# A list scheduler's model of TensorE waves, tile changes and GpSimd results is changed, with its margin and its table of moods

## The chip, the cores and the metric

The kernel runs on one NeuronCore of a Trainium2 chip. The metric is the time of one execution on the device in microseconds (us). Smaller is better. Times are medians of several executions of the same built kernel; a profile is taken of one execution.

## The reference

The input `x` has 2048 tokens of 512 numbers. Two layers follow each other, each with an attention part A and a mixer-and-MLP part B. Part A has 32 heads of 16 numbers that share one key and one value projection. Biases and gains are absent everywhere.

```python
def _A_ref(x, wq, wk, wv, wo):                     # H = 32, Dh = 16
    q = (x @ wq) -> (heads, 2048, 16); k = x @ wk; v = x @ wv
    p = softmax(q @ k.T * Dh ** -0.5)              # 32 x 2048 x 2048
    return concat_heads(p @ v) @ wo
def _B_ref(x, w1, w2, w3, w4):
    h = gelu(layernorm(x) @ w1)                    # 512 wide, four parts of 128
    hs = (parts of h shifted by +1, -1, +2, -2 tokens) @ w2
    x1 = x + hs
    return x1 + gelu(layernorm(x1) @ w3) @ w4      # 1792 wide
x = x + A(layernorm(x)); x = x + B(layernorm(x))   # twice
```

The exponentials are the largest elementwise work: 2 layers x 32 heads x 2048 x 2048 = 268 million of them.

## The kernel before

**Tiling.** Tokens are cut into 16 tiles of 128. A chunk is four tiles (512 queries); in the second layer the last chunk is cut in two of 256 queries (`CHUNKS`). Attention of a chunk is done in eight blocks of four heads, each over 16 key tiles. The unit of attention is a *half*: two heads, 512 query columns, one key tile (two key tiles for a chunk of 256), so 2 x 512 scores on 128 partitions. There are 2048 halves in the kernel.

**Two ways for a half.** `declare_unit` (L1099) has TensorE write the scores QK into two PSUM banks (L1071), and ScalarE (ACT) take the exponential of 128x1024 in one instruction, L1115, into `EA`. TensorE then multiplies it by the values (the PV product, L1194, from `EA`). Two pairs of PSUM banks are used in turn, so ACT can work on one half while TensorE fills the next. `declare_pair` (L1121) does the exponential without ACT: VectorE (DVE) turns the scores into the bits of a bf16 number by a multiplication and an addition (`J`, L1136, two per half). Two more versions with another step added (`JK`, L1146) are made by GpSimd (POOL), or by DVE when POOL already has `ADDS` of them open. The PV product then takes `J` and two `JK`, three times the PV work of a unit.

**PV on TensorE.** A PV product is four matmuls in four column strips of the array, which run side by side: one *wave*. All dense products (projections W1, W2, W3, W4, WO through `dot`, L670) are waves of four matmuls as well. QK uses row strips, and two to four QK matmuls run side by side. A change from row strips to column strips, or to the whole array, is a *tile change*.

**What sets the order.** Nothing is ordered by hand. The program first builds a list of operations with estimated durations, and the class `Plan` plays them through in its own clock: at each moment it picks, for every free engine, the ready operation of the best priority. The order that comes out is emitted as five in-order instruction streams with semaphore waits; at run time only the order is left, not the planned times. What the planner believes sits in constants and in `_place` (L321): an operation may start `LAT` (60 ns for TensorE) after its producer's planned end. TensorE's side work, which is all of it but QK and PV, starts `MARGIN` later still, and takes a freed PSUM bank only `MARGIN` after the planned end of what freed it (`_after`, L158, `_pick`, L197); QK and PV (`side=False`) have no margin. A change of kind on TensorE costs `SWITCH` (`begin`, L271). A TensorE operation of `stream` columns lasts `stream / 2400` us at the full clock. QK for ACT has priority 0 and is protected by due times (`limits`, L282); PV has 2 and, in the side work of projections and MLPs, priorities go up to 12. When TensorE's planned activity falls short, `filler` (L1077) puts in a wave of zeros, ONES times NIL (L670), which keeps the array's clock up. `pump` and `assign` decide which halves go to DVE and POOL.

**The table.** `TEMPER` has one symbol for each 12.5 us of planned time. `temper` (called by `pump`) reads it and sets eight rules of the planner (`RULES`) to one of 16 rows of `MOODS`.

**Other streams.** SP issues all DMAs; eight small ones (L1280, OT<-OS) move each finished block's output to where the output projection WO reads it. For the last three blocks of a layer TensorE does that instead (L1270). ACT also does the gelus of the mixer (L1455) and of the MLP (L1535), each between two table loads.

The names that matter below: L1115 (EA, ACT), L1071 (QK), L1194 (PV), L670 (all dense waves), L1136 and L1146 (J and JK), L1280 (block outputs by DMA), L1535 (MLP gelu).

Of the kernel before, what the change touches and what calls it, by code (L numbers as in the profile page):

```python
# [31 lines left out]
class Plan:  # L32
# [6 lines left out]

    DRAIN = {"ACT": 0.15, "DVE": 0.085, "POOL": 0.0}  # L40
    SELF = 0.035
    MARGIN = 0.15
    SWITCH = 0.097
    WINDOW = 3.4133
    WARM = 0.40
    STAY = 0.36
# [111 lines left out]
    def _after(self, p, o):  # L158
# [5 lines left out]
        if o.eng == "PE" and o.side:  # L164
            lat += self.MARGIN
        elif o.side:
# [30 lines left out]
    def _pick(self, eng, t, dense=False):  # L197
# [15 lines left out]
        for o in h:  # L213
# [6 lines left out]
            if limit and o.prio > 0:  # L220
                end = self.run_end(o, t)
                if (not joins or end > self.pe_end + 0.02) and \
                        any(end + (self.SWITCH if o.pe[0] != "Q" else 0.0) > x for x in limit):
                    continue
# [3 lines left out]
            if self.CLOSE and eng == "PE" and o.prio > 2 and o not in low and o.take is None:  # L228
                key = (self.CLOSE, o.seq)
            if stick and o.prio > 2 and o.pe[0] == self.pe_kind and not any(self.run_end(o, t) + self.SWITCH > x for x in due):  # L230
                key = (self.STICK, o.seq)
# [5 lines left out]
            if o.take is not None:  # L237
                if not all(p.placed and (p.end <= t + 1e-9 or p.eng == "PE") for p in o.take.gates):
                    continue
                margin = self.MARGIN if o.side else self.LAT["PE"]  # L240
                for i, (ft, b) in enumerate(self.pool):
# [29 lines left out]
    def begin(self, o, t):  # L271

        if o.pe[0] != self.pe_kind:
            return max(t, self.pe_end + self.SWITCH)
        if len(o.pe) == 3:
# [32 lines left out]
    def lend(self, banks, o):  # L308

        for b in banks:  # L310
            self.pool.append((o.end, b))
            self.pool_last[b] = o
        heapq.heappush(self.events, o.end + self.MARGIN)

# [6 lines left out]
    def _place(self, o, t):  # L321
        o.start = t
        o.placed = True
        if o.port and o.eng == "POOL" and o.dur > 0.5:
            x = self.order["DVE"][-1] if self.order["DVE"] else None
            if x is not None and x.port and x.start <= t < x.start + self.RACE and len(self.order["DVE"]) > 1:
                o.preds.add(self.order["DVE"][-2])
        self.left -= 1
        o.pos = len(self.order[o.eng])
        self.order[o.eng].append(o)  # L330
        if o.dma:
            s = max(t + 0.61 * (o.parts - 1) + 1.4, self.dma_free)
            o.end = s + o.dma / 330e3 + 0.6
            self.dma_free = s + o.dma / 330e3
            self.free_at[o.eng] = t + 0.63 * o.parts
        elif o.eng == "PE":
            self.roll(t)
            kind, stream, act = o.pe[0:3]
            f = 2400.0 if self.warm else 1200.0
            o.start = t = self.begin(o, t)  # L340
            end = t + stream / f
            if kind != self.pe_kind:
                self.lane = [t] * 4
            for x in (o.pe[3] if len(o.pe) > 3 else range(4)):
                self.lane[x] = end
            self.pe_kind = kind
            self.pe_end = max(self.pe_end, end)
            o.dur = end - t
            o.end = end + 0.17
            self.free_at["PE"] = t + 0.015 if len(o.pe) > 3 else end  # L350
            heapq.heappush(self.events, self.pe_end)
            self.roll(self.pe_end)
            self.activity[-1] += act
            self.debt += self.KEEP * 2400.0 * (self.pe_end - self.debt_at) - act
            self.debt = min(max(self.debt, -self.CREDIT * 2400.0), self.CAP * 2400.0)
            self.debt_at = self.pe_end
        else:
            wait = 0.0
            if o.port:
                if o.eng == "DVE":  # L360
                    if self.port > t + 0.07:
                        wait = max(0.0, self.port + min(o.dur, self.BODY) - t - o.dur)
                    self.port = t + wait + o.dur
                else:
                    if o.dur > 0.5:
                        wait = max(0.0, self.port - 0.06 - t)
                    else:
                        wait = max(0.0, self.port - t)
                    self.port = t + wait + o.dur - (0.08 if o.dur > 0.5 else 0.0)
            self.free_at[o.eng] = t + wait + o.dur  # L370
            o.end = t + wait + o.dur - o.after + self.DRAIN[o.eng]
        heapq.heappush(self.events, self.free_at[o.eng])
        if o.give is not None:
            self.pool.append((o.end, o.give.bank))
            self.pool_last[o.give.bank] = o
            heapq.heappush(self.events, o.end + self.LAT["PE"])
            heapq.heappush(self.events, o.end + self.MARGIN)
        if o.feeds is not None and self.attach is not None:
            self.attach(o)
        for s in o.succ:  # L380
            s.npend -= 1
            r = self._after(o, s)
            if r > s.ready:
                s.ready = r
            if s.npend == 0:
                self._push(s)
        o.succ = None
# [112 lines left out]
def t_ps(n):  # L500
    return 0.066 + n * 1.043e-3


def t_x4(n):
    return 0.068 + n * 0.26e-3
# [18 lines left out]
class Kernel:  # L524
# [52 lines left out]
        (0.55, 3.0, 1.5, 3.0, 0.7, 1.2, 3, 6),  # L577
        (0.57, 2.0, 1.0, 2.0, 0.45, 1.0, 3, 4),
    )
    TEMPER = "9332e03ff77e3fffe9027e99e39c23f70e32017eeecfd1e2e715170b07f0d0890399f73cf77e47e749020d9f11791007e2af395f7507bce5"  # L580

    def __init__(self, nc, ins, out):
        self.stretch = -1
# [493 lines left out]
    def filler(self):  # L1077
# [4 lines left out]
        L = None  # L1082
        if self.main_done or dep is not None and not (dep.placed and dep.end + self.pl.MARGIN <= self.pl.now):
            if not any(t + self.pl.MARGIN <= self.pl.now for t, b in self.pl.pool):
                return
# [35 lines left out]
    def declare_pair(self, g):  # L1121

        op = self.pl.op
        m = self.ndve
        self.ndve += 1
        self.waiting.append(m)
        js = m % self.N_J
        J = self.J[:, js, :]  # L1130
        for i in range(2):
            h = 2 * g[5] + i
            L = Late()
            op("PE", lambda e, h=h, L=L: self.qk(e, g, h, L.bank), reads=self.inputs(g), writes=[L],
               pe=("Q", 512, 128, (h,)), prio=0.5, side=False, take=L)
            o = op("DVE", lambda e, i=i, L=L: e.tensor_scalar(  # L1136
                out=J[:, i * 512:(i + 1) * 512], in0=self.PB[:, L.bank, :],
                scalar1=128 * LOG2E * 0.25, scalar2=float(127 * 128), op0=ALU.mult, op1=ALU.add),
                writes=[L, ("J", js, i)], dur=t_ps(512), prio=1, side=False, give=L)
        jt = [("J", js, 0), ("J", js, 1)]  # L1140
        es = [(J, jt)]
        for k in (1, 2):
            r = (2 * m + k - 1) % self.N_JK
            self.adds = [p for p in self.adds if not p.placed]
            eng = "POOL" if len(self.adds) < self.ADDS else "DVE"
            x = op(eng, lambda e, k=k, r=r: e.tensor_scalar(  # L1146
                out=self.JK[:, r, :], in0=J, scalar1=float(self.STEPS[k]), scalar2=1.0, op0=ALU.add,
                op1=ALU.mult),
               reads=jt, writes=[("JK", r)], dur=t_x4(1024) if eng == "DVE" else 1.12, prio=2, side=False, port=True)
            if eng == "DVE":  # L1150
                o = x
            else:
                self.adds.append(x)
            es.append((self.JK[:, r, :], [("JK", r)]))
        self.pairs.append(o)
        self.add_pv(g, [(self.shaped(ap.bitcast(dt.bfloat16), [2, 512]), tg, k, m) for k, (ap, tg) in enumerate(es)])
# [136 lines left out]
    def temper(self, now):  # L1293
# [3 lines left out]
        self.stretch = w  # L1297
        mood = self.MOODS[int(self.TEMPER[w], 36) if w < len(self.TEMPER) else 0]
        for name, v in zip(self.RULES, mood):
# [302 lines left out]
```

## Time and profile before

| | us |
|---|---|
| median of 5 runs | 1506.49 |
| lowest and highest of the 5 | 1502.97 and 1508.63 |
| the profiled execution | 1506.16 |
| its span from first to last instruction | 1504.4 |
| TensorE busy (PE) | 1482.1 |
| ScalarE busy (ACT) | 1436.9 |
| VectorE busy (DVE) | 1335.1 |
| GpSimd busy (POOL) | 1218.0 |

A group of instructions is written as line, engine, operation, output<-input, shapes and number, then busy time and the mean length of one in ns, then how long the engine had been idle just before such instructions and which producer ended most of that idle time. In a timeline each row is a run of equal instructions: start, length, engine, line, and in brackets the idle time ahead of it with what ended it. Two cautions: matmuls are pipelined, and the record of a short one is longer than the time it occupies; and a row that merges several ACT instructions ends with the last one's end.

### The profile page before, as it was taken

The numbers are of one execution on the slowest core, as the hardware profiler recorded it, in microseconds if no ns is written. First come the engines' busy times: TensorE is split into PE (matmuls) and PEld (weight loads), VectorE is DVE, ScalarE is ACT, GpSimd is POOL, SyncE is SP. The second block draws the span as 40 slices with busy tenths as digits, with TensorE's granted clock in tenths as the row PEclk, the third lists the DMA queues.
The fourth block names the chain that finished last, engine by engine and source line by source line (L and its number), as shares of the span: only waits on it lengthen the run. The fifth ranks groups of instructions, "written<-read, shape, count | busy, mean of one in ns | idle before, by whom it ended". The sixth has DMA issues, their size and how long they took to land.

```text
span 1504.4 us, 63139 instructions
## 1 busy us (share of the span) xinstructions
PE 1482.1 (99%) x28473; PEld 652.2 (43%) x28473; DVE 1335.1 (89%) x2396; ACT 1436.9 (96%) x1519; POOL 1218.0 (81%) x1280
## 2 busy tenths in 40 slices
PE   9999999999999999999999999999999999999999
PEld 4444333444444444444444344444443435454555
DVE  8899999988999999998786899999799999898873
ACT  7999999999999999999989999999999999998962
POOL 3899989888899878998655797889789998787851
PEclk9999999999999999999999999999999999999999
DMA  6100100001000000100000000010000000000000
GB/s 212 29 6 6 20 6 6 6 3 21 5 6 5 5 7 5 19 4 2 2 3 3 2 9 9 7 20 5 13 14 8 5 6 14 14 11 8 8 14 24
DMA packets 32142, 21.50 MB, mean 14 GB/s; under 512 B 12672, under 2 KB 31360, under 8 KB 31872
## 3 DMA queue, kind: packets, MB, share of 16 engines
q1 hardware_dynamic: 31872, 17.47, 4.8%
q8 instruction: 222, 3.64, 1.0%
q14 instruction: 48, 0.39, 0.1%
HBM read 7.90 MB, written 2.10 MB: 7 GB/s over the span
## 4 chain that ended last, share of the span: by engine, by line
PE 53%; ACT 38%; DVE 6%; POOL 1%; issue 1%; DMA 0%
ACT EA L1115 37%; PE PB L1071 17%; PE PB L1194 17%; PE PB L670 16%; DVE J L1136 3%; PE PB L867 1%; POOL JK L1146 1%; ACT G L1535 1%; DVE ST L785 1%; PE PB L1000 1%; PE PB L1251 1%; DVE JK L1146 0%; PE PB L1236 0%; ACT L1115 0%; DVE Y L822 0%
## 5 line engine op out<-in xcount | busy, mean ns | idle before, releaser
L1115 ACT ACTIVATE EA<-PB 128x1024 bf16<-128x1024 f32 x1429 | 1323.3, 1074 | 13.2 <-PE PB L1071 9.7
L1146 POOL TENSOR_SCALAR JK<-J 128x1024 uint16<-128x1024 uint16 x1019 | 1081.2, 1061 | 191.7 <-DVE J L1136 95.8
L1136 DVE TENSOR_SCALAR J<-PB 128x512 uint16<-128x512 f32 x1238 | 796.3, 680 | 74.4 <-PE PB L1071 70.1
L1071 PE MATMUL PB<-QT,KT 32*128 32x512 bf16 (+1 forms) x4608 | 606.4, 360 | 6.7 <-ACT EA L1115 3.5
L1194 PE MATMUL PB<-EA,VP 128*32 128x256 bf16 (+1 forms) x6432 | 373.0, 264 | 1.3 <-DVE ACCF L1224 0.2
L1194 PE MATMUL PB<-JK,VD 128*32 128x256 bf16 (+1 forms) x5568 | 321.4, 265 | 2.7 <-POOL JK L1146 1.4
L1071 PEld LDWEIGHTS PB<-QT,KT 32*128 32x128 bf16 x4608 | 160.8, 91 | 358.6 <-ACT EA L1115 226.5
L1194 PEld LDWEIGHTS PB<-EA,VP 128*32 128x32 bf16 x6432 | 154.6, 95 | 131.1 <-issue 100.0
L1194 PEld LDWEIGHTS PB<-JK,VD 128*32 128x32 bf16 x5568 | 126.8, 94 | 155.6 <-issue 92.0
L1194 PE MATMUL PB<-J,VD 128*32 128x256 bf16 (+1 forms) x2784 | 174.2, 263 | 0.8 <-DVE J L1136 0.7
L670 PE MATMUL PB<-ZT,W 128*32 128x512 bf16 (+2 forms) x2816 | 167.8, 342 | 0.4 <-DVE ZT L876 0.2
L1146 DVE TENSOR_SCALAR JK<-J 128x1024 uint16<-128x1024 uint16 x219 | 149.9, 690 | 5.0 <-PE PB L1194 3.6
L670 PE MATMUL PB<-W,G 128*32 128x512 bf16 x1624 | 102.5, 380 | 0.1
L1194 PEld LDWEIGHTS PB<-J,VD 128*32 128x32 bf16 x2784 | 68.0, 95 | 38.1 <-issue 26.8
L1530 DVE CAST G<-PB 128x512 bf16<-128x512 f32 (+2 forms) x126 | 72.4, 581 | 12.2 <-PE PB L670 10.5
L670 PE MATMUL PB<-ONES,NIL 128*32 128x512 bf16 x800 | 75.0, 394 | 2.7 <-DVE J L1136 1.9
L670 PEld LDWEIGHTS PB<-ZT,W 128*32 128x32 bf16 x2816 | 65.1, 96 | 28.9 <-issue 16.1
L1535 ACT ACTIVATE G<-G 128x1792 bf16<-128x1792 bf16 x29 | 47.0, 1686 | 21.6 <-DVE G L1530 21.6
L805 POOL TENSOR_TENSOR SM<-SM,MH 128x2 f32<-128x2 f32 (+1 forms) x69 | 50.2, 729 | 21.4 <-DVE SM L807 10.5
L670 PEld LDWEIGHTS PB<-W,G 128*32 128x32 bf16 x1624 | 39.0, 96 | 37.1 <-issue 8.7
L1257 DVE TENSOR_TENSOR OS<-ACCF,PB 128x512 bf16<-128x512 bf16 (+1 forms) x72 | 44.4, 617 | 4.4 <-PE PB L1251 3.9
L1511 POOL TENSOR_TENSOR X<-Y,X 128x512 f32<-128x512 bf16 x32 | 37.6, 1180 | 8.5 <-DVE Y L1493 6.0
(108 smaller groups left out, 842.5 us busy)
## 6 DMA issues: line engine op xcount, KB each, us to landing
OT<-OS SPq DMA_DIRECT2D x424, 8.0 KB, 1.8
W<-in_B_w_dram SPq DMA_DIRECT2D x2, 1792.0 KB, 15.0
X<-in_A_x_dram SPq DMA_DIRECT2D x8, 256.0 KB, 4.9
QT<-QS SPq DMA_DIRECT2D x32, 64.0 KB, 2.5
out_dram<-OUTB SPq DMA_DIRECT2D x16, 128.0 KB, 1.7
OT<-OS SPq DMA_DIRECT2D x104, 4.0 KB, 1.8
W<-in_B_w_dram SPq DMA_DIRECT2D x2, 512.0 KB, 9.7
WQ<-in_A_wq_dram SPq DMA_DIRECT2D x1, 512.0 KB, 4.5
```

Source lines behind the costliest of these rows:

```text
L670: ins = e.matmul(self.PB[32 * g:32 * g + 32, bank, 0:n], lhsT=lhsT[:, 32 * g:32 * g + 32], rhs=rhs, start=start, stop=stop, tile_position= ...
L785: op("DVE", lambda e, tb=tb: e.bn_stats(self.ST6[:, tb, :], src(tb)), reads=[tagf(tb)], writes=[("ST", tb)], dur=0.606, prio=prio)
L805: op("POOL", lambda e: e.tensor_tensor(out=out, in0=src, in1=self.MH[:, 0, a:b], op=ALU.pow), reads=tags + [("MH",)], writes=tg(r), dur=0. ...
L1071: ins = e.matmul(self.PB[:, bank, j * n:(j + 1) * n], lhsT=self.KT[32 * h:32 * h + 32, la, (kb + j) * 128:(kb + j + 1) * 128], rhs=self.QT ...
L1115: o = q.feeds = op("ACT", lambda e: e.activation(self.EA[:, ea, :, :], self.PB[:, b0:b0 + 2, :], ACTF.Exp, scale=0.25), writes=bk + [("EA" ...
L1136: o = op("DVE", lambda e, i=i, L=L: e.tensor_scalar(out=J[:, i * 512:(i + 1) * 512], in0=self.PB[:, L.bank, :], scalar1=128 * LOG2E * 0.25 ...
L1146: x = op(eng, lambda e, k=k, r=r: e.tensor_scalar(out=self.JK[:, r, :], in0=J, scalar1=float(self.STEPS[k]), scalar2=1.0, op0=ALU.add, op1 ...
L1194: ins = e.matmul(self.PB[32 * x:32 * x + 32, self.ACC, p * hw:p * hw + hw], lhsT=v[:, la, kb + j, :], rhs=ap[:, i, j * w + u * hw:j * w + ...
L1257: op("DVE", lambda e: e.tensor_tensor(out=osm, in0=acc, in1=self.PB[:, M.bank, 0:n], op=ALU.mult), reads=am, writes=[M] + om, dur=t_ps(n), ...
L1511: op("POOL", lambda e, tb=tb: e.tensor_tensor(out=self.X32[:, tb, :], in0=self.Y[:, tb % 6, :], in1=self.X32[:, tb, :], op=ALU.add), reads ...
L1530: op("DVE", lambda e, f=f, L=L: e.tensor_copy(self.G2[:, f, 0:n], self.PB[:, L.bank, 0:n]), writes=[L] + [(x, f, i) for x in ("G2", "GE") ...
L1535: op("ACT", lambda e, i=i: e.activation(self.G2[:, :, i * 128:(i + 1) * 128], self.G2[:, :, i * 128:(i + 1) * 128], ACTF.Gelu_apprx_tanh), ...
```

## The change

Four constants or terms of the planner change, and the table.

- A PV or other column-strip operation (kind "P") lasts 6 ns longer in the plan for every 512 columns begun (`WAVE`).
- A tile change costs 103 ns in the plan in place of 97 (`SWITCH`).
- The margin kept ahead of TensorE's side work, and before side work uses a freed PSUM bank or a lent one comes in, falls from 150 to 90 ns (`MARGIN`).
- The result of a `JK` on GpSimd counts as ready 70 ns before the planned end of the instruction (`after`); DVE's `JK` is as before.
- `TEMPER` is another string, of 113 symbols in place of 112; past its end the first row of `MOODS` holds.

The arithmetic, the tiles, the buffers and the operations themselves are not touched; only their order and the choice between units, pairs, POOL and DVE can differ.

```diff
-    MARGIN = 0.15
-    SWITCH = 0.097
+    MARGIN = 0.09
+    SWITCH = 0.103
+    WAVE = 0.006
...
             kind, stream, act = o.pe[0:3]
             f = 2400.0 if self.warm else 1200.0
             o.start = t = self.begin(o, t)
-            end = t + stream / f
+            end = t + stream / f + (self.WAVE * ((stream + 511) // 512) if kind == "P" else 0.0)
...
-    TEMPER = "9332e03ff77e3fffe9027e99e39c23f70e32017eeecfd1e2e715170b07f0d0890399f73cf77e47e749020d9f11791007e2af395f7507bce5"
+    TEMPER = "8033ee39ee377177e2fc0e03ec3fe7470c0ad17fee0e5df7ee7330e00050000a42037e4ce5591f07513f43f3fee2df192097e373cc00f03c4"
...
-               reads=jt, writes=[("JK", r)], dur=t_x4(1024) if eng == "DVE" else 1.12, prio=2, side=False, port=True)
+               reads=jt, writes=[("JK", r)], dur=t_x4(1024) if eng == "DVE" else 1.12, prio=2, side=False, port=True,
+                   after=0.0 if eng == "DVE" else 0.07)
```

## The prediction, as put on record before the run

> **What bounds the kernel now.** I read the page first. PE is busy for 99% of the span, ACT for 96%.
>
> ```profile
> PE 1482.1 (99%) x28473; PEld 652.2 (43%) x28473; DVE 1335.1 (89%) x2396; ACT 1436.9 (96%) x1519; POOL 1218.0 (81%) x1280
> ...
> L1115 ACT ACTIVATE EA<-PB 128x1024 bf16<-128x1024 f32 x1429 | 1323.3, 1074 | 13.2 <-PE PB L1071 9.7
> ...
> L670 PE MATMUL PB<-ONES,NIL 128*32 128x512 bf16 x800 | 75.0, 394 | 2.7 <-DVE J L1136 1.9
> ```
>
> PE's 99% can't be taken at its word: 800 of its matmuls are 200 waves of zeros, put in where the planner saw room. ACT's 96% is real work. So I read ACT's timeline next, for where ACT stands still.
>
> ```profile
> 34.55 192.01 ACT L1115 ACTIVATE EA<-PB 128x1024 bf16<-128x1024 f32 x209 [0.66 <-PE PB L1071]
> ...
> 776.96 1.28 ACT L1535 ACT_TABLE_LOAD   x1
> 785.65 4.87 ACT L1535 ACTIVATE G<-G 128x1792 bf16<-128x1792 bf16 x3 [7.41 <-DVE G L1530]
> ...
> 794.82 16.30 ACT L1115 ACTIVATE EA<-PB 128x1024 bf16<-128x1024 f32 x17 [1.05 <-PE PB L1071]
> 812.13 7.53 ACT L1115 ACTIVATE EA<-PB 128x1024 bf16<-128x1024 f32 x8 [1.02 <-PE PB L1194]
> ...
> 1375.48 1.03 ACT L1115 ACTIVATE EA<-PB 128x1024 bf16<-128x1024 f32 x1 [3.22 <-PE PB L1071]
> ...
> 1384.02 60.11 ACT L1115 ACTIVATE EA<-PB 128x1024 bf16<-128x1024 f32 x64 [0.48 <-PE PB L1194]
> 1444.15 1.28 ACT L1455 ACT_TABLE_LOAD   x1
> ```
>
> From 34.55 to 1444.15 ACT stands still in two places only: at the change of layer (7.41 + 1.05 + 1.02 = 9.5 us) and near 1375 (3.22, then 0.72, 0.50 and 0.48: 4.9 us). After the last exponential come 60 us in which PE works alone.
>
> There is a third loss that the brackets don't show. Where nothing is late, exponentials start 0.906 us apart: in two narrow windows of the same view the first start is at 102.63 and at 107.16, five starts later (4.53 / 5).
>
> ```profile
> 102.63 5.67 ACT L1115 ACTIVATE EA<-PB 128x1024 bf16<-128x1024 f32 x6
> ...
> 107.16 6.65 ACT L1115 ACTIVATE EA<-PB 128x1024 bf16<-128x1024 f32 x7
> ```
>
> The 209 above take 192.01 / 209 = 0.919 each. Start by start, 762 of about 1400 are within 1 ns of 904; 218 are 41 to 300 ns later, together 21.5 us; another 338 are 2 to 20 ns later, 5.3 us, mostly right behind a late one. The late ones are late QKs. For 167 of the 218 (15.8 us) no wait of PE on DVE or POOL lies in the time before: PE simply came round too late. The other 51 (5.6 us) follow a PE wait, on POOL's JK above all (3.1 us).
>
> [...] The trace has this run of 26 waves:
>
> ```profile
> 729.04 5.79 PE L670 MATMUL PB<-W,G 128*32 128x512 bf16 x104
> ```
>
> Less one lone wave of 0.394 that is (5.79 - 0.394) / 25 = 0.216[...]. So the old plan, with 213.3, is 2.5 ns short per wave, and the new one, with 219.3, 3.5 long. A tile change costs 0.10 (QK start at 602.56, PV at 602.88, less 0.213), so 97 and 103 are both near. [...] the mean clock granted is 0.51 only from about 1375 to 1378, right behind PE's stall at 1371.
>
> **The change, part by part.** The built orders can be counted. Durations are those above; the sum is made against the profiled 1506.16, which is 0.3 below the median.
>
> (a) Work. EA goes from 1429 to 1430: +0.9 us on ACT. DVE gets 3 JK at 0.690 more and 2 J at 0.680 less, POOL 5 JK less: under 6 us, beside ACT, no cost. PE has 8 PV waves, 8 runs of QK and 41 waves of zeros less (200 to 159). At 0.216 the zeros are 8.9 us of PE time. By themselves they gain nothing, as ACT bounds; they count in (e). If ACT's cover were gone, the 8.9 would be the gain.
>
> (b) Change of layer. ACT's order tells it. Before: chunk 2's gelu G x4, EA x13, last chunk's GP gelu, EA x27, G x3, EA x27, G x2. After: GP, EA x1, G x4, EA x2, G x3, EA x31, G x2, with 21 EA more ahead of GP. So chunk 2's W4 now falls between G x4 and G x3. PE must do, from the first of the four gelus: 56 waves W4 (12.1 us), 56 waves W3 of 384 columns (9.1, at 0.163 from the run of 224 in the before trace, 9.28 long), 20 transposes with their tile changes (1.5), 9 PV (1.0), and DVE 0.8 for the last eviction: 24.5. ACT has meanwhile 4.85 of gelu, two table loads (2.56), two EA (1.84): 9.3. It stands still 15.2, against 9.5: **+5.7**. Bounds: 0 (PE work overlaps the gelu more than I see) to +9.
>
> (c) The stall near 1375. It is a WO that waits for block outputs by DMA:
>
> ```profile
> 1374.21 0.62 PE L670 MATMUL PB<-WO,OT 128*32 128x512 bf16 x8 [3.26 <-issue]
> ```
>
> and SP's queue shows why:
>
> ```profile
> 1323.26 49.73 SPq L1280 DMA_DIRECT2D OT<-OS  x64
> ```
>
> All eight blocks of the chunk sit in one queue: 64 issues at 0.78 us, where the plan counts 0.63. In the old order four of these blocks end within two halves of each other. In the new one the eight ends are some 7 to 13 us apart, and a block needs 8 x 0.78 = 6.2 us of SP; WO comes about 15 us after the last end. So the stall goes: **-4.9**. What is late next there is nothing that I find; bounds -4.9 to -2.
>
> (d) The end. Columns that PE must still stream after the last QK: 134,408 before, 141,320 after (80 more matmuls of chunk 2's W3, fewer W1 and PV). 6912 / 2400 = **+2.9**. PE has no slack there (56.0 us of streaming in the 61.8 that were left). Bounds +1 to +4.
>
> (e) Late QKs. WAVE and SWITCH make the plan charge for time that PE does need, so fewer side waves go ahead of a QK than fit. I take two thirds of the 15.8 away (-10.5) and of the small ones -2.0. Against it: JK of POOL has no margin at all. Before, the plan has it usable 1.12 + 0.06 = 1.18 after its start; now 1.11; in the trace it is 1.047 long and the waiting weight load starts 0.053 later: 1.10. The slack falls from 80 to 10 ns, while POOL's pitch in the trace is 1.125 to 1.175. I let the 3.1 us behind POOL double: +3.1. What queues behind a waiting PV is all of PE: the next QK, and behind it ACT. MARGIN concerns side work only; a DVE result then has 0.685 + 0.06 + 0.09 = 0.835 in the plan against 0.680 + 0.053: still 100 ns to spare, no cost; bounds 0 to +2. Net **-9.4**, bounds -19 to +8.
>
> Sum: 0.9 + 5.7 - 4.9 + 2.9 - 9.4 = -4.8. 1506.2 - 4.8 = 1501.4, or 1501.7 against the median; I say **1501.5**, by itself 1495 to 1503.4. A difference under 0.2% (3 us) is about what this measurement can't tell from none.
>
> **Rivals.**
> *Given back.* The late QKs lose only about 5 us and just pay for (b) and (d): 1506. For it: part (e) is the only large gain that is not a single event. Against: 15.8 us is precisely PE being later than planned.
> *Slower, by POOL.* PV waits for JK in order. If the waits behind POOL grow by more than 2 x 3.1 while the late ones without a wait fall by less than a third (-5), (e) is above +1 and the sum +5.6 or more: 1512, up to 1517. It decides from the point where (e) is above -1.6, the sum being then +3. For it: PE already waits for POOL often, with 80 ns of slack.
>
> ```profile
> PEld PB L1194 <- POOL JK L1146: 39.5, 153, 0.6
> ```
>
> Against it: each such wait is 0.26 us with the tile change in it, and most don't reach ACT.
> *It does not do what it says.* The plan now overcharges waves by 3.5 ns, so PE runs ahead of plan and the new table was fitted to a slower PE; ACT's starts stay as they are: 1506.2 + 4.6 = 1510.8.
>
> **How the numbers follow.** Forecast (faster) 0.50; given back 0.20; slower by POOL 0.17; not as said 0.13. Range 1492 to 1513: it takes in the bounds of (b) and (e) and most of the two slower cases. Faster 0.50, same 0.20, slower 0.30.
>
> **What would show it.** (a) 1430 EA. (b) One bracket of 13 to 17 us before the G x3 near 790, in place of 7.41. (c) No WO waiting on issue near 1375, SP's runs of L1280 of 8 to 16. (d) 62 to 65 us from the last EA to the end. (e) Mean pitch in long runs of EA at 0.910 to 0.914 in place of 0.919, and the wait of L1194 for POOL above 39.5. A pitch still at 0.919 makes the forecast wrong, and so does a half-clock stretch, since 41 waves of zeros are gone.

## The result and the profile after

| | before | after |
|---|---|---|
| median, us | 1505.46 (46 runs, 1502.89 to 1508.63) | 1502.34 (26 runs, 1502.05 to 1503.24) |
| ratio, 95% interval | | 0.998 (0.9975 to 0.9985) |
| the profiled execution | 1506.16 | 1502.23 |
| its span | 1504.4 | 1500.3 |
| exponentials on ACT (EA) | 1429 | 1430 |
| waves of zeros | 200 | 159 |

The change makes the kernel 3 us (0.2%) faster, and its times lie closer together (why is told under e2). In the code after, lines are one higher than before from L43 on and two higher from about L1152 on: QK is L1072, EA L1116, PV L1196, dense waves L671, JK L1147, the MLP's gelu L1537.

The groups of the page after, in the order in which those of before were shown:

```profile
PE 1477.9 (99%) x28277; PEld 654.5 (44%) x28277; DVE 1329.3 (89%) x2397; ACT 1429.8 (95%) x1520; POOL 1213.7 (81%) x1275
...
L1116 ACT ACTIVATE EA<-PB 128x1024 bf16<-128x1024 f32 x1430 | 1316.3, 1145 | 5.4 <-PE PB L1072 3.1
```

The shares of busy time say nothing of the gain. The idle time in the last line does: ACT was idle ahead of exponentials for 13.2 us before, for 5.4 after. ACT's timeline shows where it still stands:

```profile
769.28 1.28 ACT L1537 ACT_TABLE_LOAD   x1
786.22 4.87 ACT L1537 ACTIVATE G<-G 128x1792 bf16<-128x1792 bf16 x3 [15.66 <-DVE G L1532]
...
794.83 10.46 ACT L1116 ACTIVATE EA<-PB 128x1024 bf16<-128x1024 f32 x11 [0.48 <-PE PB L1072]
806.80 16.60 ACT L1116 ACTIVATE EA<-PB 128x1024 bf16<-128x1024 f32 x18 [1.51 <-PE PB L1196]
...
1375.32 56.19 ACT L1116 ACTIVATE EA<-PB 128x1024 bf16<-128x1024 f32 x61
1431.95 5.61 ACT L1116 ACTIVATE EA<-PB 128x1024 bf16<-128x1024 f32 x6 [0.44 <-PE PB L1196]
1437.58 1.28 ACT L1457 ACT_TABLE_LOAD   x1
```

The bracket at the change of layer has grown from 7.41 to 15.66 us. The stall near 1375 is gone: 61 exponentials run through it without a bracket. The next table load after the last exponential comes at 1437.58, not at 1444.15.

What the brackets don't show is the lateness of single starts. Over the whole kernel I took, for each exponential that follows another, how much more than 904 ns lies between the two starts, and summed what is under 300 ns. Call this the lateness. It fell from 29.3 to 19.2 us, and the starts that are 41 to 300 ns late fell from 218 to 135. The view of waits gives the same from PE's side. Its columns are the total in us, the number of waits and the longest. These are the weight loads of QK that wait for ACT to give a bank back, that is, QKs that are early. First before, then after:

```profile
PEld PB L1071 <- ACT EA L1115: 226.5, 743, 0.8
...
PEld PB L1194 <- POOL JK L1146: 39.5, 153, 0.6
```

```profile
PEld PB L1072 <- ACT EA L1116: 295.1, 1006, 0.8
...
PEld PB L1196 <- POOL JK L1147: 38.9, 152, 0.5
```

QK waits for ACT 1006 times instead of 743: PE is in front of ACT more often. PE's waits for POOL are unchanged.

The two profiled executions differ by 3.9 us, their spans by 4.0. The parts, from the two traces:

| part | us |
|---|---|
| first exponential starts at 13.51, not 14.18 | -0.7 |
| three brackets near its start, 1.56 in place of 2.21 | -0.6 |
| one exponential more | +0.9 |
| change of layer: 15.66 + 0.48 + 1.51 in place of 7.41 + 1.05 + 1.02 + 0.42 | +7.7 |
| from 1370 to the last exponential: 0.44 in place of 3.22 + 0.72 + 0.50 + 0.48 | -4.5 |
| lateness, 19.2 in place of 29.3 | -10.1 |
| from the last exponential to the end, 62.8 in place of 60.2 | +2.5 |
| not placed | +0.8 |
| sum | -4.0 |

The lateness that is won (-10.1) and what is lost at the change of layer and at the end (+7.7 and +2.5) cancel. What is left is about the size of the stall that went.

### The profile page after: what moved, and what is told of

Its sections match the earlier page's. It is cut to its first block, busy times and chain, and to the rows that moved or that the text cites. A ratio compares the mean times of both kernels' runs of the same rounds, so it can differ in the third digit from the quotient of the medians.

```text
span 1500.3 us, 62760 instructions
## 1 busy us (share of the span) xinstructions
PE 1477.9 (99%) x28277; PEld 654.5 (44%) x28277; DVE 1329.3 (89%) x2397; ACT 1429.8 (95%) x1520; POOL 1213.7 (81%) x1275
## 4 chain that ended last, share of the span: by engine, by line
ACT 70%; PE 24%; DVE 4%; POOL 1%; issue 0%; POOLq 0%
ACT EA L1116 67%; PE PB L671 10%; PE PB L1072 6%; PE PB L1196 6%; DVE J L1137 2%; ACT G L1537 1%; POOL JK L1147 1%; ACT L1116 1%; PE PB L868 1%; ACT GP L1457 1%; DVE JK L1147 1%; PE PB L925 0%; ACT L1457 0%; ACT L1537 0%; DVE G L1532 0%
## 5 line engine op out<-in xcount | busy, mean ns | idle before, releaser
L1116 ACT ACTIVATE EA<-PB 128x1024 bf16<-128x1024 f32 x1430 | 1316.3, 1145 | 5.4 <-PE PB L1072 3.1
L1147 POOL TENSOR_SCALAR JK<-J 128x1024 uint16<-128x1024 uint16 x1014 | 1077.1, 1062 | 167.3 <-DVE J L1137 82.5
L1072 PE MATMUL PB<-QT,KT 32*128 32x512 bf16 (+1 forms) x4608 | 610.3, 359 | 12.3 <-ACT EA L1116 6.1
L1196 PE MATMUL PB<-EA,VP 128*32 128x256 bf16 (+1 forms) x6448 | 370.1, 263 | 1.4 <-DVE ACCF L1230 1.0
L1072 PEld LDWEIGHTS PB<-QT,KT 32*128 32x128 bf16 x4608 | 163.3, 91 | 375.0 <-ACT EA L1116 295.1
L1196 PE MATMUL PB<-JK,VD 128*32 128x256 bf16 (+1 forms) x5536 | 318.9, 266 | 2.5 <-POOL JK L1147 1.5
L1196 PEld LDWEIGHTS PB<-EA,VP 128*32 128x32 bf16 x6448 | 154.8, 95 | 121.3 <-issue 93.7
L1196 PEld LDWEIGHTS PB<-JK,VD 128*32 128x32 bf16 x5536 | 126.8, 94 | 151.9 <-issue 91.8
L1196 PE MATMUL PB<-J,VD 128*32 128x256 bf16 (+1 forms) x2768 | 175.3, 264 | 0.2 <-DVE J L1137 0.2
L671 PE MATMUL PB<-ZT,W 128*32 128x512 bf16 (+2 forms) x2816 | 167.6, 342 | 0.7 <-DVE J L1137 0.2
L1147 DVE TENSOR_SCALAR JK<-J 128x1024 uint16<-128x1024 uint16 x222 | 143.9, 654 | 3.2 <-PE PB L1196 1.0
L671 PE MATMUL PB<-W,G 128*32 128x512 bf16 x1624 | 103.1, 380 | 0.1
L1196 PEld LDWEIGHTS PB<-J,VD 128*32 128x32 bf16 x2768 | 67.8, 95 | 42.1 <-issue 34.5
L671 PEld LDWEIGHTS PB<-ZT,W 128*32 128x32 bf16 x2816 | 65.1, 96 | 33.0 <-issue 17.0
L1537 ACT ACTIVATE G<-G 128x1792 bf16<-128x1792 bf16 x29 | 47.0, 1686 | 32.7 <-DVE G L1532 32.6
L806 POOL TENSOR_TENSOR SM<-SM,MH 128x2 f32<-128x2 f32 (+1 forms) x69 | 49.2, 716 | 21.0 <-DVE SM L808 10.1
L671 PE MATMUL PB<-ONES,NIL 128*32 128x512 bf16 x636 | 58.1, 401 | 0.1
L671 PEld LDWEIGHTS PB<-W,G 128*32 128x32 bf16 x1624 | 41.4, 96 | 34.3 <-issue 9.2
```

The source lines that it names most:

```text
L671: ins = e.matmul(self.PB[32 * g:32 * g + 32, bank, 0:n], lhsT=lhsT[:, 32 * g:32 * g + 32], rhs=rhs, start=start, stop=stop, tile_position= ...
L806: op("POOL", lambda e: e.tensor_tensor(out=out, in0=src, in1=self.MH[:, 0, a:b], op=ALU.pow), reads=tags + [("MH",)], writes=tg(r), dur=0. ...
L1072: ins = e.matmul(self.PB[:, bank, j * n:(j + 1) * n], lhsT=self.KT[32 * h:32 * h + 32, la, (kb + j) * 128:(kb + j + 1) * 128], rhs=self.QT ...
L1116: o = q.feeds = op("ACT", lambda e: e.activation(self.EA[:, ea, :, :], self.PB[:, b0:b0 + 2, :], ACTF.Exp, scale=0.25), writes=bk + [("EA" ...
L1147: x = op(eng, lambda e, k=k, r=r: e.tensor_scalar(out=self.JK[:, r, :], in0=J, scalar1=float(self.STEPS[k]), scalar2=1.0, op0=ALU.add, op1 ...
L1196: ins = e.matmul(self.PB[32 * x:32 * x + 32, self.ACC, p * hw:p * hw + hw], lhsT=v[:, la, kb + j, :], rhs=ap[:, i, j * w + u * hw:j * w + ...
```

## The experiments

The theory is that of the prediction: the constants let PE come to its QKs in time, the change of layer and the end give much of it back, and the stall near 1375 goes because the output projection WO no longer waits for the SP queue, which issues the DMAs. The rivals are that the new table was only a luckier order, that POOL's waits take part of the gain, and that the zeros matter. Experiments e1 to e4, e7 and e8 keep the order on every engine, so that only the named cost changes. In e5, e6 and e9 to e12 the planner runs with other constants and gives another order.

### The constants or the table: e5 and e6

The two diagonals of the change: the constants of after with the table of before, and the reverse.

```diff
-    MARGIN = 0.15   SWITCH = 0.097   (no WAVE, JK of POOL after=0.0)
+    MARGIN = 0.09   SWITCH = 0.103   WAVE = 0.006, JK of POOL after=0.07
     TEMPER of before                                      # e5; e6: the reverse
```

> The constants of after (margin 0.09, tile change 0.103, wave 0.006, POOL's JK 0.07 later) with the table of before. The program it builds has 1448 exponentials on ACT (before 1429), so the time must be about 19 x 0.92 = 17 us above before plus whatever the side work stalls: 1520 to 1550. The time is not the question, the lateness of starts is. Theory (the constants make the QKs come in time, whatever the table): lateness under 300 ns, summed over all starts of exponentials, near that of after, 18 to 22 us, with 120 to 150 starts 41 to 300 ns late. Rival (the new table was simply a luckier order, the constants do nothing to the lateness): near that of before, 27 to 31 us with 200 to 230 late starts.

> The constants of before with the table of after, the other diagonal. It builds with 1456 exponentials on ACT, 27 more than before: 25 us above before plus stalls, 1525 to 1550. Theory (constants make the lateness): 27 to 31 us of lateness under 300 ns and 200 to 230 starts 41 to 300 ns late, as before. Rival (the table makes it): 18 to 22 us and 120 to 150, as after.

Both are slower: e5 1568.47 us, ratio 1.0418 (1.04 to 1.0437), e6 1535.84 us, ratio 1.0205 (1.0188 to 1.0222). e5 is further off than expected: beside 19 exponentials more, ACT's brackets above 0.3 us between 35 us and the last exponential sum to 54.9 us against 14.8 before. But the lateness follows the constants: 19.6 us with 131 late starts in e5, 32.1 us with 243 in e6, which is a little above the 31 and 230 that were named for it. The waits of QK for ACT say the same, e5 first:

```profile
PEld PB L1072 <- ACT EA L1116: 286.5, 981, 0.8
```

```profile
PEld PB L1071 <- ACT EA L1115: 229.2, 735, 0.8
```

981 is like after's 1006, 735 like the 743 of before, whichever table is used. For the lateness the theory holds, and the luckier order falls; these two runs don't say whose doing the other parts of the ledger are. What the table does is another thing: it fits one set of constants, and with the other set the plan takes 19 or 27 more exponentials on ACT. e5 also stalls more (the 54.9 us above), e6 does not (13.4). So the time of a change of one part alone measures mainly the misfit.

### Which constant: e9 to e12

Each changes one of the four in the kernel before, with the old table.

```diff
+    WAVE = 0.006                                          # e9
-    SWITCH = 0.097
+    SWITCH = 0.103                                        # e10
-    MARGIN = 0.15
+    MARGIN = 0.09                                         # e11
-    dur=t_x4(1024) if eng == "DVE" else 1.12, prio=2, side=False, port=True)
+    dur=..., port=True, after=0.0 if eng == "DVE" else 0.07)   # e12
```

> The kernel before with WAVE alone (6 ns more per column-strip wave in the plan), old table. It builds with 1470 exponentials on ACT, so its time is 38 us above before plus stalls, 1540 to 1580; read is the lateness of starts (before 29.3 us under 300 ns, 218 starts 41 to 300 ns late). Theory, as in step (e) of the prediction: WAVE is the larger of the two corrections and brings most of what both constants bring, 20 to 24 us and 130 to 180 late starts. Rival (the margin does it): 27 to 31 us, 200 to 230.

> The kernel before with SWITCH alone (tile change 0.103 in place of 0.097), old table; 1471 exponentials on ACT, 1540 to 1580 us. Theory, as in step (e): it takes part of the lateness away, less than WAVE: 24 to 28 us, 180 to 210 late starts. Rival (it does nothing): 29 to 31 us.

> The kernel before with MARGIN alone (0.09 in place of 0.15), old table; 1470 exponentials on ACT, 1540 to 1580 us. Step (e) gave the margin no cost and no gain (0 to +2 us): 29 to 31 us of lateness, 210 to 235 late starts. Rival (side work that starts earlier leaves the QK's way sooner): 20 to 25 us. Second rival (the smaller margin puts PE behind DVE more often): above 33 us.

> The kernel before with the earlier result of POOL's JK alone (0.07), old table; 1468 exponentials on ACT, 1540 to 1580 us. Step (e) had the waits behind POOL double: PE's waits for POOL from 39.5 to 60 us or more and the lateness from 29 to 32 us or more. Rival (the waits behind POOL are as they were, because POOL's instruction itself is 1.05 to 1.07 where the plan has 1.12): 36 to 43 us of waits for POOL, lateness 28 to 30 us.

One execution each. The expectations had counted ACT's table loads with the exponentials; the traces have 1453 to 1457.

| kernel | time, us | lateness, us | starts 41 to 300 ns late | waits of QK for ACT | PE waits for POOL's JK, us |
|---|---|---|---|---|---|
| before | 1506.16 | 29.3 | 218 | 743 | 39.5 |
| e9 WAVE | 1556.77 | 23.1 | 138 | 930 | 40.3 |
| e10 SWITCH | 1554.56 | 23.4 | 163 | 882 | 26.5 |
| e11 MARGIN | 1553.87 | 32.0 | 243 | 712 | 32.6 |
| e12 POOL | 1552.29 | 30.1 | 227 | 714 | 41.0 |
| e5 all four | 1569.6 | 19.6 | 131 | 981 | 41.1 |
| after | 1502.23 | 19.2 | 135 | 1006 | 38.9 |

WAVE takes 6.3 us of lateness away and SWITCH 5.9; MARGIN adds 2.7 and POOL's term 0.8. Their sum, -8.7, is near the -9.7 of e5, so the four nearly add up. How far can one such number be trusted? The order of before was profiled twice more with other parts cut (e1, e2): 28.0 and 28.6; that of after once more (e3): 18.6. So one order varies by about 1 us from run to run. A new order is a new draw, and the table alone shows how wide that is: e6 has the constants of before and 2.8 us more lateness than before, e5 those of after and 0.4 us more than after. The 6 us of WAVE and of SWITCH are outside of this. The 2.7 of MARGIN and the 0.8 of POOL's term are not, so neither is shown to cost anything. WAVE came out as expected; SWITCH as strong as WAVE, where less was expected; MARGIN a little above the range named for it; and in e12 the waits for POOL did not double.

### The zeros: e1

In the kernel before, the last 175 of the 200 waves of zeros stream 32 columns instead of 512.

```diff
+        z = 512 if self.nfill < 25 else 32
...
-            "PE", lambda e: self.dot(e, ..., 512, self.NIL, self.ONES,
+            "PE", lambda e: self.dot(e, ..., z, self.NIL, self.ONES[:, 0:z],
```

> The kernel before with its order untouched; of the 200 waves of zeros the last 175 stream 32 columns instead of 512. PE gets back about 175 x 0.19 = 33 us, spread over the run. Theory (ACT bounds, and a QK is late because PE comes round late): the zeros stand where PE had room, so only a part of the late QKs profits. The 21.5 us of late starts fall to 15 to 19, the time by 2 to 5 us, 1501 to 1504. Rival 1 (the zeros keep the clock up): half-clock stretches appear and the time rises by over 3 us. Rival 2 (late QKs have nothing to do with how full PE is): within 1 us of the kernel before.

The 0.19 us per wave is an estimate. The trace of before has 0.216 us for a wave of 512 columns and, at L943, 0.27 us for a row of 4 matmuls of 128x32 and 0.47 for one of 12, so 0.025 for each more; the difference is 0.19. A wave of 32 columns was not timed by itself.

1517.83 us median (1507.28 to 1521.73), ratio 1.008 (1.0066 to 1.0094). The profiled execution is the quickest of them, with a mean granted clock of 0.995 where that of the kernel before has 0.999. It has four stretches at half clock of about 3.4 us each, where the kernel before has one of 3.41 (0.50 from 1374.94 to 1378.35). This is one of the four, in the view of windows (busy us of PE, PEld, DVE, ACT and POOL, then the granted clock):

```profile
100.00:106.00 6.00, 5.27 (x82) 2.08 (x86) 5.99 (x11) 6.00 (x8) 5.56 (x6) 1.00 0.03 6
106.40:109.80 3.40, 3.40 (x51) 1.16 (x43) 2.49 (x5) 2.78 (x4) 3.16 (x4) 0.50 0.02 5
```

At half clock ACT is busy 2.78 of 3.40 us, ahead of it 6.00 of 6.00. The late starts (41 to 300 ns) fell only from 21.5 to 20.4 us in sum, where 15 to 19 was expected. So the first rival came true, the zeros keep the clock up: the mean granted clock is 0.979 to 0.995 in the six executions of e1, and 0.996 to 1.000 in the ten of the kernel before beside them. Their PE time was not what made QKs late: the 41 waves that the change drops explain next to nothing of the -10.1. e5 says the same from the other side, as it has 270 waves of zeros and a lateness of 19.6 us.

### The stall near 1375: e2

In the kernel before, every second of the 64 output DMAs of the second layer's first chunk of 256 queries is left out.

```diff
-                 for p in range(2) for i in range(2) for u in range(2)],
+                 for p in range(2) for i in range(2) for u in range(2) if (la, c, u) != (1, 3, 1)],
```

> The kernel before with its order untouched; for the chunk of the second layer whose 64 output DMAs stood in one queue, every second DMA is left out (half of that chunk's attention output is not moved), while the plan still counts eight. Theory: SP's queue is what WO waited for, so the 3.26 us wait of WO near 1374 goes, with it the half-clock stretch and the four brackets of ACT there: 4 to 5 us less, 1500.5 to 1501.5. Rival (WO stood in the order ahead of something else, a bank or a tile): the wait stays and the time moves by less than 1 us.

1500.95 us (1500.61 to 1501.27) where the kernel before took 1505.25 beside it: ratio 0.9971 (0.996 to 0.9983), -4.3 us. ACT's timeline of e2 has no stall left there (the bracket of 0.48 stays), and the trace no stretch at half clock:

```profile
1365.89 12.08 ACT L1116 ACTIVATE EA<-PB 128x1024 bf16<-128x1024 f32 x13
1378.45 1.94 ACT L1116 ACTIVATE EA<-PB 128x1024 bf16<-128x1024 f32 x2 [0.48 <-PE PB L1195]
```

WO's wait for SP's queue made the stall, and the half clock followed from it. With this one stall gone, the old order is 1.4 us under the median of the kernel after.

The half clock also goes with the spread of the kernel before. Beside the experiments it ran 22 times, each with its mean granted clock. The two executions at 1.000 took 1502.93 and 1503.63 us, those at 0.999 took 1504.10 to 1506.52, and those at 0.996 to 0.998 took 1506.45 to 1508.11. All executions of e2 and of the kernel after were at 1.000. So against an execution of the kernel before at the full clock the change gains about 1 us; the rest of its 3.1 us comes with the half clock that is gone.

### The change of layer: e3

In the kernel after, the W4 products of four tiles of the first layer (7 to 10) leave out 6 of their 14 terms, 5.2 us of PE work.

```diff
-                    for f in (2 * h, 2 * h + 1):
+                    for f in (2 * h, 2 * h + 1) if not (la == 0 and 7 <= tb <= 10) or h == 6 else (2 * h,):
```

> The changed kernel with its order untouched; in the first layer the W4 products of tiles 7 to 10 leave out 6 of their 14 terms: 24 waves less, 24 x 0.2158 = 5.2 us of PE work less, between G x4 and G x3. Theory: PE's work sets the 15.66 us for which ACT stands still there, so the bracket falls to about 10.5 and the time by 4.5 to 5.5 us, to 1497 or 1498. Rival (DVE's evictions or the layernorm chain with POOL set the end of the bracket): it stays above 14 and the time moves by less than 1.5 us.

```profile
784.32 4.87 ACT L1537 ACTIVATE G<-G 128x1792 bf16<-128x1792 bf16 x3 [13.86 <-DVE G L1532]
```

1499.77 us (1499.71 to 1499.78), 2.6 us under after; the bracket falls from 15.66 to 13.86 only. Neither expectation fits: 10.5 if PE sets the bracket, under 1.5 us in time if DVE does. PE's timeline in the kernel after, with the last eviction by DVE, shows how the bracket ends:

```profile
780.80 0.60 PE L671 MATMUL PB<-W,G 128*32 128x512 bf16 x8
781.23 4.07 PE L671 MATMUL PB<-ZT,W 128*32 128x384 bf16 x96
785.24 0.84 PE L868 MATMUL PB<-IDENT,QS 128*128 128x128 bf16 x12
...
785.64 0.55 DVE L1532 CAST G<-PB 128x384 bf16<-128x384 f32 x1
```

From 761.41 on PE goes through W4 (input G) and W3 (input ZT) without a wait in this view. The last 24 waves of W3 are over when the transposes begin, at 785.24; the last eviction starts 0.4 us later, and ACT at 786.22. The view of the chain puts the last 5.2 us on DVE, because DVE has no idle time from 781.03 on, but W3 runs beside it almost to the end. So PE sets the end here, but for some 0.4 us. In e3 PE has 5.2 us less to do, but now stands still for DVE on the way:

```profile
765.46 0.84 PE L868 MATMUL PB<-IDENT,ZR 128*128 128x128 bf16 x12 [1.40 <-DVE ZR L823]
...
770.58 0.40 PE L1196 MATMUL PB<-EA,VP 128*32 128x256 bf16 x8 [0.64 <-DVE QT L1214]
...
776.07 1.48 PE L671 MATMUL PB<-ZT,W 128*32 128x384 bf16 x32 [0.33 <-DVE G L1532]
```

With one more of 0.18 these are 2.6 of the 3.4 us that don't reach ACT. DVE's work, the layernorm's application (ZR) above all, comes that close behind PE's.

### Less dense work: e4

In the kernel before, every W3 product leaves out two of its four terms. This takes PE work away everywhere at once.

```diff
-                    for dc in (2 * h, 2 * h + 1):
+                    for dc in (3 * h,):
```

> The kernel before with its order untouched; every W3 product leaves out two of its four terms, so PE has half of the W3 waves. At the change of layer that is 28 of 56 waves x 0.163 = 4.6 us off the 9.5 of ACT, in the work after the last QK about 8.5 us. Theory (QKs are late because PE is behind with side work): of the 15.8 us of late starts without a wait about half goes, so -4.6 - 8.5 - 8 = -21, about 1484, and the pitch of the exponentials falls to 0.911 to 0.914 where W3 is interleaved. Rival (the late starts come from waits on POOL and DVE, or from ACT itself): pitch as before, -13, about 1492.

1493.49 us (1493.23 to 1493.94), ratio 0.9922 (0.9908 to 0.9935), -11.8 us; -21 was expected, and the rival's -13 is nearer, though the lateness, which the rival had unchanged, falls. The end takes 54.7 us in place of 60.2 (-5.5, where -8.5 was expected), the first bracket of the change of layer 5.19 in place of 7.41, and the lateness is 24.2. With less to do, PE is late 168 times in place of 218, not never. So room on PE alone makes QKs only somewhat more punctual. A plan that knows PE's time does no less: e9 and e10 each take as much lateness away (6.3 and 5.9 us) as leaving out half of all W3 work (5.1).

### What POOL's waits cost: e7 and e8

In both kernels POOL's JK, from the sixth pair on, writes half of its columns.

```diff
+            z = 512 if eng == "POOL" and m >= 5 else 1024
...
-                out=self.JK[:, r, :], in0=J, ...
+                out=self.JK[:, r, :z], in0=J[:, :z], ...
```

> The kernel before, with each JK of POOL from the sixth pair on writing 512 of its 1024 columns (the other half keeps an older pair's values), in the same order on every engine; POOL is then done some 0.5 us earlier and PE never waits for it. It measures what waiting for POOL costs. Theory (3.1 us of late exponentials stand behind POOL, and nothing else hangs on it): 3 us under before, 1502.4, and the sum of starts 41 to 300 ns late falls from 21.5 to 18.5 us. Rival (most of PE's 39.5 us of waits for POOL reach ACT by way of later QKs, which the ledger calls late without a wait): 8 to 15 us under before.

> The kernel after, with the same cut of POOL's JK from the sixth pair on (half of their columns left out), same order. Theory (behind POOL stand 1.9 us of late exponentials in after, so the new 0.07 did not raise that cost as the prediction had it, it lowered it): 2 us under after, 1500.4. The prediction's own figure (POOL's waits cost 6.2 us in after): 6 us under after, 1496. If e7 and e8 gain the same, the change did nothing to what POOL costs.

e7 takes 1500.54 us (1499.40 to 1502.27) against 1504.8 for the kernel before beside it: ratio 0.9972 (0.9961 to 0.9982), -4.3. e8 takes 1499.54 (1499.39 to 1499.73), ratio 0.9962 (0.995 to 0.9975) to the kernel before, and 2.8 under after's median. The lateness falls by 4.2 in e7 (to 25.1) and by 2.0 in e8 (to 17.2). It had been expected that PE then never waits for POOL. It still does; these waits fall from 39.5 to 22.0 us in e7 and from 38.9 to 21.7 in e8. So the same 17 us of waits are worth 4.3 us before and 2.8 after: the change has not raised what POOL costs, though the prediction had it doubled. What all of the waits cost was not measured. The cut is not clean, though: DVE's own JK, which was left alone, got quicker too. Before:

```profile
L1146 DVE TENSOR_SCALAR JK<-J 128x1024 uint16<-128x1024 uint16 x219 | 149.9, 690 | 5.0 <-PE PB L1194 3.6
```

and in e7:

```profile
L1147 DVE TENSOR_SCALAR JK<-J 128x1024 uint16<-128x1024 uint16 x219 | 101.0, 467 | 5.5 <-PE PB L1195 4.4
```

The same instruction takes 467 ns in place of 690, while J (L1136), which reads PSUM, stays at 680 and 683. In e8 it is 469 in place of 654. So a part of e7's and e8's gain may come by way of DVE. How large it is was not tested.

## Why the forecast held, step by step

The forecast was 1501.5, faster; the median is 1502.3. The step down was smaller than forecast, 3.1 us and not 5: the first five executions of the kernel before had a median of 1506.49, all 46 one of 1505.46. By the steps of the prediction:

**(a) Work.** 1430 exponentials, as said. That the 41 waves of zeros gain nothing by themselves is shown by e1, with the addition that narrowing them costs much.

**(b) Change of layer.** Predicted a bracket of 15.2, measured 15.66, and made of what the sum said. Counted from the end of the first of the four gelus (759.55 + 6.46 / 4 = 761.17), PE was to be busy for 23.7 us and DVE for 0.8 after it; in the trace PE is through with W3 after 24.1 (at 785.24), and ACT starts 1.0 later. In all the term is +7.7 where +5.7 was said, because the step put nothing for the brackets behind the gelu (0.48 and 1.51; before, 0.42 beside those that it counted). What the sum doesn't say, e3 does: DVE is so close behind that 5.2 us less of PE shorten the bracket by 1.8.

**(c) The stall near 1375.** Predicted -4.9, measured -4.5, and e2 confirms the mechanism. The sub-claim, that SP's runs would be short (8 to 16), is wrong. From 1306 us on they are of 32, 16, 8 and 48 DMAs. Two of them from SP's timeline in the kernel after:

```profile
1306.59 24.14 SPq L1282 DMA_DIRECT2D OT<-OS  x32
...
1368.84 47.70 SPq L1282 DMA_DIRECT2D OT<-OS  x48
```

The 32 still take 24.14 / 32 = 0.75 us each. WO comes at 1379.47 in the new order and finds what it needs:

```profile
1379.47 0.62 PE L671 MATMUL PB<-WO,OT 128*32 128x512 bf16 x8
```

The stretch at half clock, named as a sign against the forecast, didn't come either, though 41 waves of zeros are gone.

**(d) The end.** +2.9 predicted, +2.5 measured (62.8 us, within the 62 to 65 named).

**(e) Late QKs.** Predicted -10.5 - 2.0 + 3.1 = -9.4, measured -10.1. The gain is by WAVE and SWITCH, as said: e9 and e10 sum to -12.2 where the step had -12.5. As its two thirds were a guess, so close a fit is luck. The 2.5 ns that a wave was too short in the old plan are 215.84 ns, from the run of 26 waves in the trace of before, less 213.33. By size, the starts that are 41 to 300 ns late lose 8.7 us (21.5 to 12.9) and the smaller ones 1.5. Against the gain the step had POOL's term at 3.1 and the margin at nothing; e12 shows 0.8 and e11 2.7, both within what another order does (2.8 in e6). So the step had a cost for POOL that isn't seen. The reason given for POOL, that a slack of 10 ns in place of 80 must double the waits, is refuted: they are 38.9 us after, 41.0 in e12, against 39.5. Whether the smaller margin makes QKs later at all stays open.
The sign named for (e) also missed by a little: the long run of exponentials that starts at 33.82 has a mean pitch of 0.917 (220 in 201.77 us), not 0.910 to 0.914; before it was 0.919. The gain is spread over the kernel unevenly, and one row is a poor measure of it.

**The rivals.** *Given back* had (e) at -5; it is twice that, but the pay-back by (b) and (d), +10.2, is real and is why 0.2% is all that is left. *Slower, by POOL* falls by e7 and e8 together and by e12. *It does not do what it says* falls by e5 and e6: with either table the constants move the lateness from about 30 us to about 19.

**Open.** Is what is given back a price of the constants or an accident of this order? ACT's brackets above 0.3 us between 785 and 850 us sum to 17.7 us after and 20.0 in e5 (9.04, 9.32, 0.89, 0.78), and to 9.9 before and 8.4 in e6 (3.16, 1.08, 3.01, 1.17). From the last exponential to the end it is 62.8 and 68.2 with the new constants, 60.2 and 59.1 with the old. So both orders made with the four new constants lose more there, which points to a price; but e5 stalls more in many places, and two orders of each kind don't decide it. A table that keeps the change of layer at its old 9.9 us would, by the ledger above, be some 7.7 us faster than after, near 1494.6. This is an estimate; no such table was run. Nor was the old set of constants with a table searched anew.

## What to carry to other kernels

Where a planner only leaves its order behind, judge its constants by how punctual the bounding engine's starts are, over all starts, and not by the time of one build: a few ns per wave and per tile change took away 6 us of lateness each here, in one order each, and could be read although each of these builds was 45 us slower or more. Have a second order with the same constants beside it, to see what the order alone does (up to 2.8 us here). A schedule parameter that was searched under one set of constants must be searched again under another, so changes of one part alone show the misfit first. When a gain of 10 us ends as 3, list the stalls of both kernels by place: here the change of layer and the end had taken back 10, and the removal of one stall (e2) was worth as much as the whole change. Where a chain names one engine as the last, look what runs beside it: the 5.2 us of DVE at the change of layer stood over PE's work.

## What the runs showed of the hardware

- Waves of zeros could not be made cheap here: with 32 columns in place of 512 in 175 of them the median rose by 12.6 us (1517.83 against 1505.25 beside it), with four stretches at half clock in the quickest execution. PE was not at rest ahead of the one that the view under e1 shows: from 100 to 106 us its records cover 5.27 of 6.00 us, at a granted clock of 1.00.
- A stall of PE of 3.26 us cost ACT about 4.4: 3.22 at once, and 0.72 and 0.50 in the stretch of 3.41 us at half clock behind it. Without the stall, e2 is 4.3 us faster, and these three brackets are gone.
- DVE's JK of 128x1024 takes 690 ns beside POOL's full JK and 467 ns beside its half.
